# Row 0 of a fused attention and feed-forward kernel: the first half of the queries goes to the feed-forward layer ahead of the second half's masks, exponentials and last scores

## The chip, the core and the metric

The kernel runs on one core of a Trainium2 chip. The metric is the device time in microseconds (us) of one launch. The core has a matrix engine (TensorE, here PE), a vector engine (VectorE, DVE), a scalar engine (ScalarE, ACT), GpSimd (POOL) and SyncE (SP); the last two issue most of the DMA transfers here. Each engine takes its instructions in the order in which they were written, and waits on semaphores for the others.

## What is computed

The reference is attention with two kinds of masks, followed by a two-layer feed-forward network with a squared ReLU:

```python
B, H, S, D = 8, 8, 576, 64
scores = q @ k.transpose(0, 1, 3, 2) / sqrt(D)
rel = pos[:, None] - pos[None, :]
mask_plain = (rel >= 0) & (rel < 32)                       # heads 0 to 3
mask_dil = (rel >= 0) & (rel < 128) & (rel % 4 == 0)       # heads 4 to 7
attn = softmax(where(mask, scores, -1e9))
x = (attn @ v).transpose(0, 2, 1, 3).reshape(B * S, H * D) # 4608 tokens of 512
out = maximum(x @ w_in, 0) ** 2 @ w_out                    # 512 -> 2048 -> 512
```

## The kernel before

The attention works row by row of the batch (8 rows of 576 queries), the feed-forward part in chunks of 512 tokens. Nothing is scheduled by a planner: the order of the calls in the source is the order of the instructions on each engine. While one chunk goes through the feed-forward layers, the next row's attention is woven in between by `pump(n)`, which advances a generator of feed-forward work by n small steps. In the first layer two steps are one tile: four matmuls of 128x288 or 128x512 into one PSUM bank (line 291), a ReLU by ACT into `rt` (line 300), and a square by DVE into `g` (line 314 for row 0).

Row 0 has no chunk before it, so its attention stands alone, in the lines around 911 to 966. It is done in halves: the first 288 queries and the last 288. `mm1_first_gen` runs the first layer on row 0 in the same halves: eight tiles on the first half (tiles 0 to 7, which read columns 0 to 287 of `xr`), then eight on the second half, from tile 8 on, and so forth, 32 tiles in all.

The steps of row 0, with the lines that the profile names:

- Scores and exponentials: PE adds a bias that masks (`bias_of`, line 631, two matmuls of 128x288) to the scores (`s_sliding_one`, line 638, six matmuls), and `softmax` (line 619) has ACT write the exponential into one of eight units of `AT`. `s_first(hp, half)` does all three for two sliding heads and one half of the queries. Units 0 to 3 are the sliding heads, by pair of heads and half: (0,0), (0,1), (1,0), (1,1). Units 4 to 7 are the dilated heads; 4 and 6 are the first half, 5 and 7 the second. The exponentials of 5 and 7 are masked afterwards by two DVE products (line 940).
- Products with V: `av_dilated(0, t, a, ...)` (line 720, eight matmuls) gives half t of two dilated classes; `av_sliding(0, xs, m, ...)` (line 693, four matmuls for each m) gives blocks of 96 queries, m = 0 to 2 for the first half and 3 to 5 for the second. After each, DVE normalises from PSUM: a reciprocal (line 676) and a product (line 677) into `y` or `x`. V itself is cast by POOL (lines 218, 222, 235).
- Transposes: `x_dilated` (line 757) and `x_sliding` (line 742) turn a half of `y` and `x` by PE into PSUM, and ACT copies it into `xr` (lines 760 and 749, two copies each). The first layer's matmuls read `xr`: `x_sliding` is the last thing that a half needs.

PSUM is one tile of eight banks. `bank()` hands out banks 0 to 3 in turn (the first layer's tiles), `pair()` hands out pairs of banks in turn from the list `pairs`, for all of the attention. Row 0 uses all four pairs until the first layer begins; from there on the attention has only pairs 2 and 3 (banks 4 to 7):

```python
    pairs[:] = [2, 3]
    turns["pair"] = 0
    pending.append(mm1_first_gen())
    turns["bank"] = 2
```

A pair is written again only after whoever read its last content is done. The loads of `w_out` are issued by POOL (`load_w_out`, line 197), behind the casts and loads that POOL has before them; the two that the change's lines hold keep their place there.

## Time and profile before

| What | Value |
|---|---|
| Median of 3 runs | 299.29 us (298.81 to 299.5) |
| Profiled execution | 299.97 us, of which the span is 298.2 us |
| Granted PE clock, mean | 1.00 |
| Busy: PE, DVE, ACT, POOL | 96%, 68%, 59%, 33% |
| DMA | 45.59 MB, mean 153 GB/s |
| First tile of the first layer starts | 19.59 us |
| First layer runs without a gap | 22.96 to 36.68 us |

All times inside a profile count from the start of the span of one profiled execution; the launch takes about 1.8 us more than the span. In a line of the timeline the first number is the start, the second the time from the first start to the last end of the group; what stands in brackets is the idle time of the engine just before it, and what ended it. A line of the chain of waits gives the start, the duration, and the work or wait that held up the end. PE's matmuls are pipelined, so the rows of neighbouring matmuls overlap.

### The profile page before, as it was taken

To read this page: it belongs to the slowest core of one execution; us is meant where nothing else is said; L and a number is where in the kernel's file an instruction comes from. 1 tells how busy PE (TensorE), PEld (TensorE's weight loads), DVE (VectorE), ACT (ScalarE), POOL (GpSimd) and SP (SyncE) were. 2 spreads that over 40 slices of the span, in tenths; PEclk is the share of its full clock that TensorE was granted. 3 is DMA by queue.
4 is the path that set the end of the run, shared out by engine and by line. 5 is a ranking of instruction groups with operands and counts; after the bars stand their busy time and mean duration, and the time that the engine had idled before them with its cause. 6 is when DMAs were issued, how large, how long until landed. Compare 5 with 4: busy or idle time off the path is not lost.

```text
span 298.2 us, 7125 instructions
## 1 busy us (share of the span) xinstructions
PE 287.3 (96%) x2880; PEld 203.0 (68%) x2880; DVE 202.5 (68%) x371; ACT 176.4 (59%) x331; POOL 98.0 (33%) x154
## 2 busy tenths in 40 slices
PE   3999999999999999999999999999999999999995
PEld 2779854555555587646889987558755875785584
DVE  7786646778734898499588967896779624723652
ACT  1668854878538774857555648564766166425611
POOL 8492019406707245560655029209400000000000
PEclk9999999999999999999999999999999999999999
DMA  7999998799699878999999899979133230003013
GB/s 128 220 201 213 213 208 169 178 181 257 137 213 253 179 157 154 209 236 200 168 217 256 154 169 194 263 179 153 73 92 24 40 143 0 0 2 142 3 35 106
DMA packets 73969, 45.59 MB, mean 153 GB/s; under 512 B 56720, under 2 KB 67600, under 8 KB 73744
## 3 DMA queue, kind: packets, MB, share of 16 engines
q1 hardware_dynamic: 66544, 31.37, 48.0%
q0 software_dynamic: 7248, 13.63, 25.7%
q8 instruction: 22, 0.36, 0.5%
q10 hardware_dynamic: 144, 0.13, 0.1%
q14 instruction: 11, 0.09, 0.1%
HBM read 36.83 MB, written 16.52 MB: 179 GB/s over the span
## 4 chain that ended last, share of the span: by engine, by line
PE 81%; DMA 7%; DVE 4%; issue 2%; POOL 2%; SPq 1%; ACT 1%; POOLq 0%
PE PS L291 38%; PE PS L443 24%; PE PS L332 9%; DMA sv<-in_v_dram 5%; PE PS L720 3%; DMA ns<-in_k_dram 2%; PE PS L693 2%; PE PS L638 2%; PE PS L653 1%; POOL vp L218 1%; PE PS L742 1%; DVE AT L623 1%; POOL vp L222 1%; ACT AT L619 1%; SPq L168 1%
## 5 line engine op out<-in xcount | busy, mean ns | idle before, releaser
L291 PE MATMUL PS<-xr,wi 128*128 128x512 f16 (+3 forms) x704 | 133.5, 341 | 0.3 <-ACT xr L749 0.3
L300 ACT ACTIVATE rt<-PS 128x512 f16<-128x512 f32 (+2 forms) x160 | 88.5, 557 | 42.6 <-PE PS L291 39.7
L291 PEld LDWEIGHTS <-wi 128*128 128x128 f16 x704 | 75.8, 113 | 38.5 <-issue 0.4
L325 DVE TENSOR_TENSOR g<-rt 128x1024 f16<-128x1024 f16 (+1 forms) x64 | 46.1, 720 | 28.5 <-ACT rt L300 28.3
L619 ACT ACTIVATE AT<-PS 128x576 f16<-128x576 f32 x64 | 38.5, 652 | 14.8 <-PE PS L638 7.3
L443 PEld LDWEIGHTS <-S 128*128 128x128 f16 x448 | 42.8, 98 | 5.8 <-issue 0.3
L443 PE MATMUL PS<-T,S 128*128 128x256 f16 x336 | 39.5, 273 | 0.0
L443 PEld LDWEIGHTS <-g 128*128 128x128 f16 x336 | 32.2, 98 | 5.3 <-issue 0.2
L332 PE MATMUL PS<-wo,g 128*128 128x512 f16 x128 | 33.1, 379 | 0.0
L235 POOL CAST vd<-sd 128x512 f16<-128x512 f32 x32 | 23.9, 769 | 23.9 <-DMA sd<-in_v_dram 21.0
L443 PE MATMUL PS<-wo,g 128*128 128x256 f16 x224 | 26.4, 273 | 0.0
L218 POOL CAST vp<-sv 128x512 f16<-128x512 f32 x24 | 16.8, 700 | 24.2 <-DMA sv<-in_v_dram 20.0
L677 DVE TENSOR_TENSOR y<-PS,rcp 72x512 f16<-72x512 f32 (+1 forms) x32 | 22.0, 686 | 1.1
L623 DVE TENSOR_TENSOR AT<-AT,maskp 128x1152 f16<-128x1152 f16 x14 | 14.8, 1057 | 9.7 <-ACT AT L619 9.7
L623 DVE TENSOR_TENSOR AT<-AT,maskd 128x1152 f16<-128x1152 f16 x14 | 11.3, 810 | 14.1 <-ACT AT L619 14.0
L222 POOL CAST vp<-sv 32x512 f16<-32x512 f32 (+1 forms) x24 | 17.0, 708 | 1.5
L677 DVE TENSOR_TENSOR x<-PS,rcp 96x512 f16<-96x512 f32 (+1 forms) x25 | 16.6, 665 | 0.9
L720 PEld LDWEIGHTS <-AT 128*128 128x128 f16 x256 | 12.1, 100 | 7.1 <-DVE y L677 1.6
L332 PEld LDWEIGHTS <-g 128*128 128x128 f16 x128 | 10.3, 97 | 8.0
L429 DVE TENSOR_TENSOR S<-g,S 128x1024 f16<-128x1024 f16 x14 | 10.7, 804 | 7.4 <-PE PS L443 7.4
L676 DVE RECIPROCAL rcp<-PS 96x8 f32<-96x8 f32 (+3 forms) x57 | 11.2, 196 | 5.2 <-PE PS L720 2.9
L443 PE MATMUL PS<-T,g 128*128 128x256 f16 x112 | 14.2, 273 | 0.0
(94 smaller groups left out, 284.5 us busy)
## 6 DMA issues: line engine op xcount, KB each, us to landing
out_dram<-c SPq DMA_DIRECT2D x12, 512.0 KB
sv<-in_v_dram SPq DMA_DIRECT2D x48, 96.0 KB, 4.9
sd<-in_v_dram SPq DMA_DIRECT2D x16, 288.0 KB
dp<-o SPq DMA_DIRECT2D x12, 288.0 KB, 3.9
wo<-in_moe_w_out_dram POOLq DMA_DIRECT2D x4, 512.0 KB, 13.7
n<-in_k_dram POOLq DMA_DIRECT2D x6, 288.0 KB, 6.5
n<-in_q_dram POOLq DMA_DIRECT2D x6, 288.0 KB, 7.3
dd<-in_k_dram POOLq DMA_DIRECT2D x6, 288.0 KB, 8.0
```

Source lines behind the costliest of these rows:

```text
L218: nc.gpsimd.tensor_copy(vp[b % 2][:, m : m + 2, :, 0:D], sv[:, m : m + 2, :, :])
L222: nc.gpsimd.tensor_copy(vp[b % 2][0:PADP, m:m1, :, 0:D], sv[P - PADP : P, m - 1 : m1 - 1])
L235: nc.gpsimd.tensor_copy(o, by_class(sd[:, t]))
L291: nc.tensor.matmul(ph[:, o : o + b - a], w_in_of(dmk, ffc), xr[:, dmk, a:b], start=(dmk == 0 and o == 0), stop=(dmk == NDM - 1 and o + b - ...
L300: nc.scalar.activation(rt, ph[:, 0:w], ACTF.Relu)
L325: nc.vector.tensor_mul(g[:, f2 : f2 + 2, o:TOKC], rt[:, :, o:TOKC], rt[:, :, o:TOKC])
L332: nc.tensor.matmul(po, g[:, ffc, o + t * P : o + (t + 1) * P], w_out_of(ffc), start=(ffc == 0), stop=(ffc == NFF - 1),)
L443: nc.tensor.matmul(po[t], lhs(j)[:, t * P : (t + 1) * P], rhs(j), start=j == 0 and not on_top, stop=j == HF - 1, skip_group_check=on_top,)
L619: nc.scalar.activation(AT[:, u + i, 0:UW], ps[:, :, 0 : UW // 2], ACTF.Exp, scale=scale)
L623: nc.vector.tensor_mul(AT[:, u : u + n, 0:UW], AT[:, u : u + n, 0:UW], mask,)
L677: nc.vector.tensor_tensor(out=x, in0=pv[:, :, :, 0:D], in1=rcp[0:w, 0:i, 0:j].unsqueeze(3).to_broadcast([w, i, j, D]), op=ALU.mult,)
L720: nc.tensor.matmul(pav[:, e, h * (D + 2) : h * (D + 2) + D + 1], AT[:, 4 + 2 * a + t, off : off + P], vd[b % 2][:, t, 2 * a + e, h, 0 : D ...
```

## The change

The order of the calls for row 0 is changed; no step is added or taken away, and the number of instructions of every kind stays as it is. The scores (0,1) are still computed before the first layer begins, but behind the first half's products and dilated transposes, and their exponential behind the first half's copies. The masks of units 5 and 7 move behind the first half's normalisations. The products of the second half, and the scores (1,1), come after the point at which the attention has only the pairs 2 and 3, between tiles of the first layer. Fourteen steps of the first layer (seven tiles) are pumped ahead of `x_sliding(0, 1)`, where there were eight (four tiles).

```diff
-    for u in (5, 7):
-        nc.vector.tensor_mul(AT[:, u, 0:UW], AT[:, u, 0:UW], maskd[:, 1])
+
     xs, ys, zs = [], [], []
     av_dilated(0, 0, 0, ys)
     s_first(1, 0)
     av_dilated(0, 0, 1, ys)
-    s_first(0, 1)
     av_sliding(0, xs, 0, 1)
     av_sliding(0, xs, 2)
     x_dilated(0, 0, ys, True)
-    s_first(1, 1)
+    s02 = pair()
+    bias_of(s02, biasp)
+    s_sliding_one(0, 0, 1, s02, True)
     x_sliding(0, 0, xs, True)
-    av_dilated(0, 1, 0, zs)
-    av_dilated(0, 1, 1, zs)
-    av_sliding(0, xs, 3)
     load_w_out(0)
     load_w_out(1)
     pairs[:] = [2, 3]
     turns["pair"] = 0
+
+    softmax(1, [s02], None)
+    for u in (5, 7):
+        nc.vector.tensor_mul(AT[:, u, 0:UW], AT[:, u, 0:UW], maskd[:, 1])
     pending.append(mm1_first_gen())
     turns["bank"] = 2
     pump(4)
+    av_dilated(0, 1, 0, zs)
+    s_first(1, 1)
+    pump(2)
+    av_dilated(0, 1, 1, zs)
+    pump(2)
+    av_sliding(0, xs, 3)
     av_sliding(0, xs, 4, 5)
+    pump(4)
     x_dilated(0, 1, zs, True)
-    pump(4)
+    pump(2)
     x_sliding(0, 1, xs, True)
```

## The prediction

> **What bounds the kernel now.** I read the shares of busy time first, then the chain that ended last, then TensorE's (PE's) idle time in stretches of 5 us, and last the timeline from 13 to 25 us, where the change lies.

> ```profile
> PE 287.3 (96%) x2880; PEld 203.0 (68%) x2880; DVE 202.5 (68%) x371; ACT 176.4 (59%) x331; POOL 98.0 (33%) x154
> ...
> PE 81%; DMA 7%; DVE 4%; issue 2%; POOL 2%; SPq 1%; ACT 1%; POOLq 0%
> ```

> PE is the bound. The stretches say where it is not: from 25 us on it idles in five of them only (4.69, 4.56, 4.90, 4.48 and 4.63 busy of 5.00, so 0.31 + 0.44 + 0.10 + 0.52 + 0.37 = 1.74 us in 270). The work moved by the change is the same before and after, so the time can only change by PE's idle time before 25 us, and by what of that is given back later. The chain of waits shows the seam: from 22.96 us the first layer runs without a gap.

> ```profile
> 18.91 0.21 DVE rcp L676
> ...
> 19.99 0.03 DVE y L677
> ...
> 20.80 0.42 DVE x L677
> ...
> 21.80 0.70 DVE x L677
> 22.50 0.04 issue
> 22.55 0.41 PE PS L742 x6
> 22.96 13.72 PE PS L291 x112
> ```

> 112 matmuls in 13.72 us are 0.1225 us each, 0.49 us for a tile of four. Tile 8, the first that needs the second half of the queries, stands at 22.96 + 16 x 0.1225 = 24.92. The timeline (start, duration) has the rows that I move:

> ```profile
> 13.35 0.60 PE L720 MATMUL PS<-vd,AT 128*128 128x65 f16 x8 [0.26 <-POOL vd L235]
> ...
> 14.83 0.65 ACT L619 ACTIVATE AT<-PS 128x576 f16<-128x576 f32 x1 [1.06 <-PE PS L638]
> ...
> 15.69 0.60 POOL L222 CAST vp<-sv 32x512 f16<-32x512 f32 x1
> ...
> 18.46 0.67 PE L720 MATMUL PS<-vd,AT 128*128 128x65 f16 x16
> 18.85 0.70 ACT L749 COPY xr<-PS 128x288 f16<-128x288 f16 x2
> 19.59 1.14 PE L291 MATMUL PS<-xr,wi 128*128 128x288 f16 x8 [0.30 <-ACT xr L749]
> 19.76 0.19 DVE L676 RECIPROCAL rcp<-PS 72x8 f32<-72x8 f32 x1
> 19.99 0.69 DVE L677 TENSOR_TENSOR y<-PS,rcp 72x512 f16<-72x512 f32 x1
> 20.28 0.90 ACT L300 ACTIVATE rt<-PS 128x288 f16<-128x288 f32 x2 [0.74 <-PE PS L291]
> 21.14 0.51 DVE L314 TENSOR_TENSOR g<-rt 128x288 f16<-128x288 f16 x2
> ```

> A normalisation (reciprocal, then product) takes 0.92 us (19.76 to 20.68); a relu 0.45; a square 0.22 to the next instruction. A group of bias and scores holds PE for 0.96 us (13.76 to 14.72). The eight matmuls at 13.35 took 0.60 us, while sixteen of that form took 0.67 at 18.46: before about 18.3 us PE runs at half rate, though the granted clock reads 1.00.

> **The first half, up to the first tile.** PE's order becomes values, all first-half products and the dilated transposes, then scores (0,1), then the sliding transposes. The third product of `av_sliding(0, 1)` needs the exponential of the scores (1,0), which ends at 15.48; PE gets there at 15.26, since the scores that lay in between have gone: 0.25 idle. `av_sliding(2)` would start at 15.8 but needs POOL's cast of the shared rows (15.69 + 0.60 = 16.29): 0.45 idle. Then its 0.22, transposes 0.47, bias and scores 0.96: 18.0. The sliding transposes (0.43) are done at 18.6, ACT's two copies (0.70, the first after 0.40) run 18.65 to 19.35, and the first tile starts at 19.1 with its first matmul and goes on at 19.4. Before it was 19.59, so the head start is 0.2 to 0.5 us. Nothing fills PE from 18.4 on; before, 20 products did. The masks of units 5 and 7 (two of 0.6 us on DVE) move to 17.7 to 18.9, where DVE is free: nothing. The exponential (0,1) follows the copies on ACT, 19.3 to 19.9, ahead of the first relu, which is not ready earlier: nothing. POOL and SP get the same instructions in the same order; the two loads of w_out that stand in the moved lines are queued behind POOL's own casts as before: nothing.

> **The second half, between the tiles.** Before, its three first products had three pairs of PSUM banks (2, 3, 0). Now they come after `pairs[:] = [2, 3]` and go round two: first dilated product on pair 2, scores (1,1) on 3, second dilated on 2, `av_sliding(3)` on 3, `av_sliding(4, 5)` on 2, then the transposes on 3 and 2. Each waits until its pair is read out, PE takes its instructions in order, and the tiles behind it wait too. Step by step:

> - Tiles 0 and 1 run to 20.3, the first dilated product (0.25) to 20.5. In DVE's order both squares stand ahead of its normalisation. The second relu ends at about 20.9, the squares at 21.2, so the normalisation runs 21.2 to 22.1.
> - PE meanwhile does scores (1,1) (about 0.5 at full rate) and tile 2, to 21.55. The second dilated product needs pair 2: 22.1. **0.55 idle.**
> - Its own normalisation, behind the square of tile 2, ends at 23.5. PE does tile 3 and `av_sliding(3)`, to 23.0; `av_sliding(4, 5)` needs pair 2: 23.5. **0.5 idle.**
> - Tiles 4 and 5, dilated transposes, tile 6, sliding transposes and tile 7 run to 26.2. ACT has, from the relu of tile 5 (24.95) on: 0.4, copies 0.65, relu 0.4, copies 0.7. It is done at 27.0, the first of the last two copies at 26.7. Only tile 7 stands between the sliding transposes and tile 8, where it was four tiles before. **0.65 idle** until tile 8 is under way, at 26.9 in effect.

> So 26.9 against 24.92: 2.0 us later. Counted the other way: idle 0.25 + 0.45 + 0.85 + 0.55 + 0.5 + 0.65 = 3.25 against 0.95 before (0.45 ahead of the first tile, 0.2, 0.3), less 0.45 because scores (1,1) now run at full rate: 1.85. I take 2.0.

> **What carries to the end.** From 36.7 us on the row-1 loads are fixed by POOL's queue and only gain slack. The 1.74 us of later idle end on DVE or ACT, which hang on PE's own progress, so I carry all; if half of it waited for data of fixed arrival, 0.9 would be absorbed and 1.1 left. The profiled execution took 299.97 us (span 298.2 and 1.8 around it); the median of the runs is 299.29 (298.81 to 299.5). 299.97 + 2.0 = 301.97; against the median, 301.3, which I predict.

> **Rival 1, slower still: the full rate comes later.** The rate changed at about 18.3 us after 3 us in which nearly all PE time was full-height products and bias matmuls; it had not changed by 13 us, although PE was 4.56 of 5 us busy from 5 on, mostly with 64-row transposes. In the new order the stretch from 15.1 to 18.5 holds 0.7 us idle, 0.9 of transposes and one bias group instead of two. If that is too little, tiles 0 and 1 run at 0.245 us a matmul (+0.98), the group after them loses some 0.4, part of it eaten by the waits: 1.0 more, 302.3. [...] On these rows I give it a third.
> [...]

> **Rival 2, faster: the head start wins.** If the first two relus and squares were done before the first dilated product (20.5), its normalisation would end at 21.5, just when tile 2 does, and the 0.55 and 0.5 would fall away; with the copies earlier by as much, tile 8 stands at about 24.6, that is -0.3: 299.0. It decides at one point: does DVE start that reciprocal before 20.7? It needs the first tile at 18.6, and ACT's copies end later. 5 in 100.

> **Rival 3, no change.** The idle time is only moved: the later waits absorb, or PE runs some groups faster than I have them, 1.5 us in all: 299.8. Also here: that the first half is not ahead at all. It speaks against both that the three waits follow from the bank order alone. 5 in 100.

> **How the numbers follow.** The forecast of 301.3 has 0.55 (of it 0.1 with part absorbed, down to 300.4), rival 1 0.35 (302.3, up to 302.9 with the scatter of the runs and a window more), rivals 2 and 3 0.05 each. The range 300.2 to 302.9 leaves out about 0.15. 0.2% (0.6 us) is about what a measurement of this kernel can tell from no change. Faster 0.05, within it 0.05, slower 0.90.

> **What would show it.** The first L291 at 19.1 to 19.4; waits of PE for DVE's y on L720 and on L693, about 0.5 each; a wait of L291 for ACT's xr on tile 8; the unbroken run of L291 shrinks from 112 to about 96 and starts near 26.9; the first L332 comes at 38.5 instead of 36.5 and everything behind is later by as much. Rival 1 shows as eight L720 in 0.6 us after 20 us. I am wrong if the second dilated product follows within 0.1 us of tile 2, or if the shift at 38 us is gone by 60.

## The result and the profile after

The changed kernel takes 302.51 us (median of 6 runs, 301.12 to 303.73), against 299.0 us (298.46 to 299.5) for the kernel before on the same chip: a ratio of 1.0104, 95% interval 1.008 to 1.0128, or 3.1 us (the medians lie 3.5 us apart). Runs that took over 1.5% longer than the fastest of their kernel are left out of medians and ratios; there are two, both of f2 (305.50 and 306.35 us). The profiled execution took 303.6 us with a span of 301.8; it is the second longest of the six, so that its profile shows more of the loss (3.6 us) than the ratio does.

PE still carries the time (the profile's first part, and the chain that ended last):

```profile
PE 290.2 (96%) x2880; PEld 203.8 (68%) x2880; DVE 203.0 (67%) x371; ACT 176.1 (58%) x331; POOL 98.6 (33%) x154
...
PE 83%; DVE 8%; DMA 5%; issue 1%; ACT 1%; POOL 0%; DVEq 0%; ACTq 0%
```

The 2880 matmuls are the same as before, and PE is busy with them for 290.2 us instead of 287.3. So by the profile's count 2.9 of the 3.6 us are matmuls that took longer, and only 0.7 is time in which PE stood idle.

The chain of waits from 12 to 46 us (start, duration, what held up the end) shows where the time went:

```profile
11.52 7.62 DMA wi<-in_moe_w_in_dram
...
19.18 2.10 PE PS L291 x8
...
22.57 1.08 PE PS L291 x4
...
28.09 0.30 ACT xr L749
...
28.74 11.80 PE PS L291 x95
40.54 0.43 PE PS L332 x2
```

The unbroken run of the first layer had 112 matmuls from 22.96 on; now it has 95 from 28.74 on, and the second layer begins at 40.54 instead of 36.68. So 3.86 us are lost ahead of it, and 3.6 of them reach the end. The second thing to see is the price of a matmul. PE's rows of the timeline:

```profile
19.18 2.10 PE L291 MATMUL PS<-xr,wi 128*128 128x288 f16 x8 [1.03 <-DMA wi<-in_moe_w_in_dram]
21.09 0.64 PE L720 MATMUL PS<-vd,AT 128*128 128x65 f16 x8
...
22.50 1.15 PE L291 MATMUL PS<-xr,wi 128*128 128x288 f16 x4
23.44 0.64 PE L720 MATMUL PS<-vd,AT 128*128 128x65 f16 x8
...
25.59 1.14 PE L291 MATMUL PS<-xr,wi 128*128 128x288 f16 x8
```

At 19.18 eight matmuls take 2.10 us, where they took 1.14 before, and take it again at 25.59. PE ran at half rate until 25.0 us; in the profile of before it had changed to full rate at 18.2. Both times are read from the spacing of the matmuls, because the profile's granted clock reads 1.00 at either rate until its first fall.

### The profile page after: what moved, and what is told of

Its sections match the earlier page's. It is cut to its first block, busy times and chain, and to the rows that moved or that the text cites. A ratio compares the mean times of both kernels' runs of the same rounds, so it can differ in the third digit from the quotient of the medians.

```text
span 301.8 us, 7121 instructions
## 1 busy us (share of the span) xinstructions
PE 290.2 (96%) x2880; PEld 203.8 (68%) x2880; DVE 203.0 (67%) x371; ACT 176.1 (58%) x331; POOL 98.6 (33%) x154
## 4 chain that ended last, share of the span: by engine, by line
PE 83%; DVE 8%; DMA 5%; issue 1%; ACT 1%; POOL 0%; DVEq 0%; ACTq 0%
PE PS L291 39%; PE PS L443 25%; PE PS L332 10%; PE PS L720 3%; DMA wi<-in_moe_w_in_dram 3%; DMA ns<-in_k_dram 2%; PE PS L693 2%; PE PS L653 2%; DVE AT L623 2%; DVE S L429 1%; PE PS L638 1%; DVE g L325 1%; ACT AT L619 1%; PE PS L742 1%; PE PS L757 1%
## 5 line engine op out<-in xcount | busy, mean ns | idle before, releaser
L291 PE MATMUL PS<-xr,wi 128*128 128x512 f16 (+3 forms) x704 | 136.3, 344 | 1.2 <-DMA wi<-in_moe_w_in_dram 1.0
L300 ACT ACTIVATE rt<-PS 128x512 f16<-128x512 f32 (+2 forms) x160 | 88.5, 557 | 45.9 <-PE PS L291 43.4
L291 PEld LDWEIGHTS <-wi 128*128 128x128 f16 x704 | 75.8, 114 | 40.7 <-DMA wi<-in_moe_w_in_dram 1.2
L619 ACT ACTIVATE AT<-PS 128x576 f16<-128x576 f32 x64 | 38.5, 652 | 14.9 <-PE PS L638 7.6
L332 PE MATMUL PS<-wo,g 128*128 128x512 f16 x128 | 33.1, 379 | 0.0
L235 POOL CAST vd<-sd 128x512 f16<-128x512 f32 x32 | 23.4, 755 | 21.5 <-DMA sd<-in_v_dram 20.9
L218 POOL CAST vp<-sv 128x512 f16<-128x512 f32 x24 | 18.3, 762 | 23.8 <-DMA sv<-in_v_dram 22.7
L677 DVE TENSOR_TENSOR y<-PS,rcp 72x512 f16<-72x512 f32 (+1 forms) x32 | 22.0, 687 | 1.1
L623 DVE TENSOR_TENSOR AT<-AT,maskp 128x1152 f16<-128x1152 f16 x14 | 13.4, 960 | 9.2 <-ACT AT L619 9.1
L720 PEld LDWEIGHTS <-AT 128*128 128x128 f16 x256 | 12.8, 102 | 7.7 <-DVE y L677 1.8
L429 DVE TENSOR_TENSOR S<-g,S 128x1024 f16<-128x1024 f16 x14 | 12.7, 946 | 7.4 <-PE PS L443 7.4
L677 DVE TENSOR_TENSOR x<-PS,rcp 96x512 f16<-96x512 f32 (+1 forms) x25 | 16.6, 666 | 0.9
L222 POOL CAST vp<-sv 32x512 f16<-32x512 f32 (+1 forms) x24 | 16.0, 668 | 1.5
L314 DVE TENSOR_TENSOR g<-rt 128x288 f16<-128x288 f16 x32 | 9.8, 308 | 9.7 <-ACT rt L300 9.5
L332 PEld LDWEIGHTS <-g 128*128 128x128 f16 x128 | 10.3, 98 | 8.0
L720 PE MATMUL PS<-vd,AT 128*128 128x65 f16 x256 | 14.2, 200 | 0.8 <-DVE y L677 0.4
(94 smaller groups left out, 287.3 us busy)
```

Source lines behind the costliest of these rows:

```text
L218: nc.gpsimd.tensor_copy(vp[b % 2][:, m : m + 2, :, 0:D], sv[:, m : m + 2, :, :])
L222: nc.gpsimd.tensor_copy(vp[b % 2][0:PADP, m:m1, :, 0:D], sv[P - PADP : P, m - 1 : m1 - 1])
L235: nc.gpsimd.tensor_copy(o, by_class(sd[:, t]))
L291: nc.tensor.matmul(ph[:, o : o + b - a], w_in_of(dmk, ffc), xr[:, dmk, a:b], start=(dmk == 0 and o == 0), stop=(dmk == NDM - 1 and o + b - ...
L300: nc.scalar.activation(rt, ph[:, 0:w], ACTF.Relu)
L332: nc.tensor.matmul(po, g[:, ffc, o + t * P : o + (t + 1) * P], w_out_of(ffc), start=(ffc == 0), stop=(ffc == NFF - 1),)
```

## The experiments

They were made to part two causes: the waits of the new order, and the late full rate. Each is compared with the kernel before on the same chip.

**Dense matmuls at the start (e1, e2, e3, e4).** All four have these lines ahead of the first load; nobody reads the result:

```diff
+    hot = S2.rearrange("p j t -> p (j t)")[:, 0:TOKC]
+    nc.vector.memset(hot, 0.5)
+    for i in range(8):
+        nc.tensor.matmul(PS[:, 6 + i % 2, :], hot[:, 0:P], hot, start=True, stop=True)
```

e1 is the old order with them:

> The old order with eight dense matmuls of 128x512 on a constant added at the start, while PE waits for its first data; nobody reads their result. They are to bring PE to full rate before its own work begins. Theory (the loss of the new order has two parts, 2.0 us from waits of PE and the rest from the full rate coming at 25.2 instead of 18.5 us): full rate well before 18 us, the unbroken run of the first layer ends about 1.0 us earlier than at 36.7, time 298.0 (0.997 of before). Rival A (the rate plays no part, all of the loss is the order): 299.0, no change. If the full rate is lost again during the transposes from 6 to 13 us, this run can't tell.

299.7 us, ratio 1.0000 (0.9986 to 1.0015). Its profile has the full rate from 17.6 us on again, so it doesn't tell the theories apart. e2 is the new order with them:

> The new order with the same eight dense matmuls at the start. Theory: the rate is full throughout, what stays is the waits of PE: about 2.0 us behind the old order with the same matmuls, so 300.0 (1.003 of before), 2 to 2.5 us less than the new order without them (302.5). Rival A (order alone): 302 to 302.5. Rival B (the rate alone makes the loss, the waits are hidden): the same time as the old order with the matmuls, 298.0.

301.35 us, ratio 1.0081 (1.0047 to 1.0115), more than the 300.0 of the theory. The busy times by stretch of its profile (length, PE busy, then the other engines; granted clock third from the right) show what the eight matmuls do:

```profile
4.40:7.70 3.30, 1.66 (x27) 0.98 (x25) 3.10 (x13) 0.00 (x0) 3.09 (x7) 0.98 1.03 175
7.90:14.50 6.60, 6.32 (x144) 4.80 (x141) 4.68 (x14) 4.85 (x8) 3.08 (x7) 0.51 1.11 223
14.70:20.00 5.30, 3.41 (x51) 2.39 (x50) 3.20 (x9) 2.91 (x7) 5.13 (x9) 1.00 1.23 199
```

They bring the full rate for one stretch, from 4.1 us on by the spacing of the matmuls; then it is lost at 7.6 us, after a stretch in which PE was busy for half the time while it waited for its next data (0.98 us for a load, 0.66 for DVE), and comes back at 14.4. In this execution the rate was full before the first tile, and still the second layer began at 38.47, that is 1.8 us later than in the profile of before: the order has a cost of its own. e3 adds a third pair of banks for the second half; `bank()` takes its turns from the list `banks` there, and both lists go back to the old ones behind `x_sliding(0, 1)`:

```diff
-    pairs[:] = [2, 3]
+    pairs[:] = [2, 3, 0]
+    banks[:] = [2, 3]
     turns["pair"] = 0
     ...
-    turns["bank"] = 2
+    turns["bank"] = 0
```

> The new order with the eight dense matmuls, and three pairs of PSUM banks for the second half's attention (pairs 2, 3 and 0, while the first seven tiles of the first layer use banks 2 and 3 alone). Takes away what makes PE wait for a pair at the second dilated product and at av_sliding(4, 5). Theory: those two waits of about 0.5 us each fall away, the wait of tile 8 for ACT's copies stays; 0.9 us less than the new order with the matmuls and two pairs, 299.1. Rival (PE waits there for DVE or ACT in another way, and the pairs don't matter): within 0.2 us of it, 300.0.

301.89 us, ratio 1.0075 (1.0058 to 1.0093): by time not to be told from e2. The two waits for DVE's y are gone from its profile, but the full rate came at 20.6 us there and at 14.4 in e2's, so the comparison mixes both causes.

e4 takes the first half of the change alone (the moved lines are shown where they now stand, not where they were taken out):

```diff
     softmax(1, [s02], None)
     ...
+    av_dilated(0, 1, 0, zs)
+    s_first(1, 1)
+    av_dilated(0, 1, 1, zs)
     load_w_out(0)
     ...
     pump(4)
     av_sliding(0, xs, 3)
     av_sliding(0, xs, 4, 5)
     x_dilated(0, 1, zs, True)
     pump(4)
     x_sliding(0, 1, xs, True)
```

> The first half as in the new order, with the eight dense matmuls; the second half's two dilated products and the scores (1,1) go back ahead of the first layer's first tile, where all four pairs are free, and four tiles stand ahead of the sliding transposes as in the old order. One part of the change alone. Theory: the second half's products are off pair 2, but the first tile starts later by the products: 0.7 us less than the whole new order with the matmuls, 299.3, and still 1.3 us behind the old order with them. Rival (the deferral of the second half makes all of the loss): as fast as the old order with the matmuls, 298.0.

301.49 us, ratio 1.0062 (1.0039 to 1.0085), where the theory had 299.3; half rate until 22.4 us in its profile. Inconclusive for the same reason as e3; h3 repeats it without the matmuls.

**Dense matmuls all along the first 13 us (f1, f2, g3).** Sixteen of 128x256 at the start and four to six ahead of seven later groups of transposes, scores and products, in a bank that is written next:

```diff
+    def dense(i, n):
+        for j in range(n):
+            nc.tensor.matmul(PS[:, i + j % 2, 0:HT], hot[:, 0:P], hot, start=True, stop=True)
+    dense(6, 16)
     load_sliding_v(0, 0, 2)
     ...
     s01 = pair()
+    dense(2, 4)
     s_dilated_one(0, 0, 1, s01)
```

f1 is the old order:

> The old order with dense matmuls of 128x256 on a constant put between row 0's first steps, all ahead of 13.3 us: sixteen at the start, then 4 to 6 at a time ahead of the transposes, scores and first products; nobody reads their result. Eight at the start alone had raised PE to full rate for one stretch of 3.4 us and then lost it. These are to hold the rate. Theory: if the rate is full from 14 us on at the latest in every run, the end of the first layer's unbroken run comes at 35.7 instead of 36.6, time 298.3 to 298.6 and less scatter between the runs than the 2 us of before; what the added matmuls cost ahead of 13.3 us is the uncertain part (0 to 0.7). Rival (the rate is lost again between them): 0.5 to 3 us slower than before, half-rate rows after 13.3 us.

300.27 us, ratio 1.0033 (1.0009 to 1.0057), slower where the theory had it faster. The rate was full from 6.4 us on in its profile, but the first product with V came at 15.0 instead of 13.35, and the second layer began at 37.79 instead of 36.68. f2 is the new order:

> The new order behind the same dense matmuls as the old order with them. Theory: with the rate held in both, what is left is the order's own cost, PE's waits: 1.9 to 2.2 us behind the old order with the same matmuls (300.3 to 300.6 if that one takes 298.4), the waits of PE for DVE's y at the second dilated product and at av_sliding(4, 5) about 0.5 each, and tile 8 for ACT's copies; scatter below 1.5 us. Rival A (the rate made the whole loss): equal to the old order with the matmuls within 0.3. Rival B (the rate made nothing of it): 3.1 us behind it, as the new order is behind the old one without the matmuls.

303.39 us (300.94 to 305.31), ratio 1.0111 (1.0078 to 1.0144). It is 2.3 us behind f1 by the ratios and 3.1 by the medians, so rival A is out, and the times alone don't tell the theory from rival B; the scatter of 4.4 us is about three times the 1.5 that was expected. The stretches of its profile show that the rate was not held:

```profile
9.60:13.00 3.40, 3.40 (x86) 2.40 (x82) 2.19 (x5) 2.49 (x4) 1.55 (x4) 1.00 1.15 208
13.00:16.30 3.30, 3.19 (x76) 2.36 (x76) 1.52 (x3) 1.68 (x3) 3.19 (x6) 1.00 1.14 212
16.30:19.70 3.40, 1.74 (x33) 1.23 (x32) 2.09 (x7) 0.96 (x3) 3.34 (x7) 0.97 1.25 206
19.80:26.50 6.70, 6.15 (x47) 3.78 (x46) 2.96 (x10) 3.13 (x7) 2.77 (x5) 0.51 1.12 214
26.60:30.00 3.40, 3.03 (x42) 2.57 (x39) 2.60 (x9) 2.38 (x8) 0.54 (x1) 1.00 1.05 206
```

PE had the full rate, was busy for only 1.74 of 3.40 us in the stretch ahead of the first tile, and lost it for 6.8 us (from 19.5 to 26.3, so the stretches as cut here end 0.2 us late), although it was busy again in 6.15 of 6.70. The old order behind the same matmuls kept it in its profile. So in this execution the full rate was not only put off but taken away. The longest gap there, 1.1 us, stands ahead of a matmul for which the profile shows no releaser. g3 has the old order and fewer of them (31; the text on record says 33):

```diff
-    dense(6, 16)
+    dense(6, 14)
     ...
     s01 = pair()
-    dense(2, 4)
+    dense(2, 2)
```

> The old order with fewer dense matmuls ahead of 13.3 us (14 at the start, then 2 to 4 at a time, 33 in all instead of 48 of 128x256). The larger dose held the full rate from 6.6 us on, but put the first product with V at 15.0 instead of 13.35 us and gave 1.0033 of before. Theory: half the dose delays it by 0.5 or less; if the rate holds, the first layer's run ends at 36.0 and the time is 298.7 (0.997 of before). Rival (too thin to hold the rate): 299.5 to 301, half-rate rows between 8 and 18 us.

302.78 us, ratio 1.0107 (1.0088 to 1.0125): the smaller dose did not hold the rate, PE was at half rate up to 16.3 us and the first product came at 16.7. As a faster kernel it came to nothing.

**Dense matmuls where the new order lets PE wait (g1, g2).**

```diff
     av_sliding(0, xs, 0, 1)
+    dense(2, 2)
     av_sliding(0, xs, 2)
     ...
     x_sliding(0, 0, xs, True)
+    dense(2, 3)
```

> The new order with five dense matmuls of 128x256 put where PE waits in it: two ahead of av_sliding(2), which waits for POOL, and three between the first half's sliding transposes and the first tile, which waits for ACT. Nobody reads their result and no other instruction moves. Theory (the new order's thin stretch from 15 to 19 us keeps PE at half rate for one or two stretches of 3.4 us more): with the stretch filled the rate comes as in the old order, by 18 to 19 us, and the time falls from 302.5 to 301.3, the waits of about 2.0 us alone (1.006 to 1.007 of before). Rival A (the rate has other causes, dense work there changes nothing): 302.5 or slower by the 0.2 that the matmuls may delay the transposes. Rival B (the waits cost nothing): 299.5.

301.55 us (300.83 to 302.25), ratio 1.0069 (1.0047 to 1.0092), as the theory had it: with five matmuls that compute nothing the changed kernel comes out 1.0 us faster, by the medians (302.51 to 301.55) and by the ratios. The two were measured apart, each against before beside it, and the intervals just overlap (1.0080 to 1.0092). The full rate came at 17.6 us in its profile. Only the first two of the five stood ahead of that, from 15.91 on; the other three began at 18.14, when PE was waiting for the weights anyway. The chain of waits has the order's cost with the rate in time:

```profile
22.67 0.70 DVE y L677
...
23.41 0.43 PE PS L693 x8
...
26.18 0.30 ACT xr L749
...
26.83 11.80 PE PS L291 x95
38.63 0.43 PE PS L332 x2
```

The second layer begins at 38.63, that is 1.95 behind before's 36.68. PE's waits in that stretch (total, times, longest) are those of the working:

```profile
PE PS L291 <- DMA wi<-in_moe_w_in_dram: 0.5, 1, 0.5
PE PS L693 <- DVE y L677: 0.4, 1, 0.4
PE PS L720 <- DVE y L677: 0.3, 1, 0.3
PE PS L291 <- ACT xr L749: 0.2, 1, 0.2
```

They count from the modelled end of the last matmul. From start to start, as the working counts, more is lost:

```profile
20.95 0.68 PE L291 MATMUL PS<-xr,wi 128*128 128x288 f16 x4
21.96 0.43 PE L720 MATMUL PS<-vd,AT 128*128 128x65 f16 x8 [0.34 <-DVE y L677]
...
22.72 0.29 PE L693 MATMUL PS<-vp,AT 128*128 128x65 f16 x4
23.41 0.43 PE L693 MATMUL PS<-vp,AT 128*128 128x65 f16 x8 [0.40 <-DVE y L677]
```

The tile at 20.95 takes 0.49 us, so the second dilated product comes 0.5 us late. Four products take 0.13 us, so `av_sliding(4, 5)` comes 0.6 us late. Tile 8 comes in two steps, its first matmul at 26.52 and the rest from 26.83 on, together 0.5 us late.

g2 is g1 with the third pair of e3:

> The same with three pairs of banks for the second half's attention (2, 3 and 0, the first seven tiles on banks 2 and 3 alone). Theory: the waits for pair 2 at the second dilated product and at av_sliding(4, 5) go, about 0.9 us less than the new order with the five matmuls: 300.4; what stays of the order's cost is tile 8 behind ACT's copies and the idle time ahead of the first tile. Rival (the pairs don't matter, DVE's chain of normalisations sets the pace of the second half with two pairs or three): within 0.3 us of it, 301.2, and the sliding transposes wait for x instead.

300.92 us, ratio 1.0047 (1.0026 to 1.0067), 0.6 us less than g1; the intervals overlap. Both waits for y are gone from the profile, and one of 0.3 us is there for what DVE does next:

```profile
PE PS L742 <- DVE x L677: 0.3, 1, 0.3
```

From the first tile to the second layer it takes 18.93 us (19.59 to 38.52) against 19.52 in g1, which fits the difference of the medians. So the bank pairs are probably a part of the cost, of about 0.6 us, though the times don't prove it. Behind them DVE sets the pace: in g2's chain it works from 22.78 to 25.54 without a pause, squares and normalisations, until the transposes can go.

**Each half of the change alone (h2, h3).** h2 is the old order up to the scores (0,1), with masks and exponentials where they were, and the new order from the pairs on:

```diff
-    s_first(1, 1)
     x_sliding(0, 0, xs, True)
-    av_dilated(0, 1, 0, zs)
-    av_dilated(0, 1, 1, zs)
-    av_sliding(0, xs, 3)
     ...
     pump(4)
+    av_dilated(0, 1, 0, zs)
+    s_first(1, 1)
+    pump(2)
     ...
```

> One part of the change alone, with no matmuls added: masks, scores (0,1), their exponential and the whole first half stand as in the old order; the second half's products, the scores (1,1) and the transposes stand as in the new one, on pairs 2 and 3, between tiles. Theory (the order's 2.0 us come from the second half's waits for pair 2 and for ACT; the late rate comes from the new first half, thin between 15 and 19 us): 2.0 us over before and no more, 301.5, with scatter like before's 2 us, and the profile shows the full rate by 19 us. Rival A (the new first half costs part of the 2.0): 300.5. Rival B (the scores (1,1) taken out of the stretch are enough to delay the rate): 302.5, like the whole change.

302.71 us (301.98 to 303.04), ratio 1.0095 (1.0069 to 1.0121): rival B. This part alone costs what the whole change costs, the late rate included (22.6 us in its profile). Without the scores (1,1) and the twenty products that stood ahead of the first tile, PE waits in the chain for DVE's x until 18.2 (0.32 us) and for ACT until 19.6 (0.49 us), and the first eight matmuls run at half rate:

```profile
18.22 0.50 PE PS L742 x4
...
19.14 0.41 ACT xr L749
...
19.59 2.14 PE PS L291 x8
```

h3 is e4 without added matmuls:

> The other part alone, with no matmuls added: the first half as in the new order, then the second half's dilated products and the scores (1,1) ahead of the first tile on all four pairs, and four tiles ahead of the sliding transposes as in the old order. Theory: the waits for pair 2 are gone, 1.2 us are left (the exponential (1,1) now comes behind ACT's copies, so av_sliding(3) and what follows it come later); 300.7 where the rate comes as before, 301.8 where it comes one stretch later, which the thin first half makes likely in some runs. Rival (the first half ahead is a gain by itself): 299.0 or less.

301.36 us, ratio 1.0051 (1.0031 to 1.0071), between the two values expected. PE waits 1.0 us for DVE's x at the dilated transposes there, and its profile has half rate until 21.9.

**A better use of a tile (h1).** The old order with one tile more ahead of `x_sliding(0, 1)`:

```diff
     x_dilated(0, 1, zs, True)
-    pump(4)
+    pump(6)
     x_sliding(0, 1, xs, True)
```

> The old order with five tiles instead of four ahead of x_sliding(0, 1) (pump(6) for the last pump(4)). PE waits there 0.3 us for DVE's last x; one tile more (0.49 us) covers that, and three tiles are left between it and tile 8, 1.5 us against the 0.7 of ACT's copies. Theory (what a pumped tile is worth depends on the wait it covers, not on its number): the unbroken run ends 0.3 us earlier, 299.3 where before takes 299.6 (0.999), hardly to be told from no change. Rival (the fifth tile delays the transposes for nothing): 0.2 us slower.

299.39 us against 299.86, ratio 0.9980 (0.9961 to 1.0000). PE's wait for x ahead of L742 is gone from the chain, and the unbroken run starts at 23.30 with 108 matmuls left, which is worth 0.15 us there; the rest of the 0.5 is within what runs differ by. It is the only version that comes out below before, and just at the edge of being told from it.

## Why the prediction was right or wrong

**The direction: right. The mechanism: right where the rate is in time.** The prediction forecast 2.0 us slower by PE's own waits, 301.3; the time is 302.51, inside the range and 1.2 above the value. The forecast is borne out by g1: the order's cost is 1.95 us in the profile and 1.0069, or 2.1 us, by the runs. Tile 8 is under way at 26.83 where the working had 26.9. The changed kernel itself lands near rival 1's 302.3. That the number lies inside the range is owed to rival 1, for which the range had been widened.

**What was mis-sized: rival 1.** The late rate was put down as a rival with a chance of a third. The runs show it as the second term of the sum: the difference between the change and g1 is 1.0 us in the medians and 1.9 in the two profiles (40.54 against 38.63; the one is the second slowest of its six runs, the other the second fastest). The sign given for it is there: eight matmuls of line 720 take 0.64 us at 21.09 and at 23.44. Five of six runs of the change lie above 302. The price of 1.0 was right for the median. That 1.0 was worked out for half rate that ends behind tiles 0 and 1 and the group after them. h2's profile has it so (22.6 us), the change's has not: there it lasted to 25.0, though PE was busy for all of the 5.82 us from 19.18 on. The "window more" at the range's upper end is a term that no run shows by itself; what the runs showed in its place is a full rate that comes 6.8 us later than before (25.0 against 18.2 in the profiles) and a median of 302.51.

e2 shows when the rate changes: it rose at 4.1 us by the spacing of the matmuls, and the granted clock, worked out from its means by stretch, fell at 7.55 and rose at 14.38, so the changes lie 3.4 and 6.8 apart. The full rate that lasts comes at another time in each kernel's profile (14.4 us in e2, 17.6 in g1, 18.2 in before, 20.6 in e3, 25.0 in the change); that the scatter of the runs has its cause there is not shown. f2 lost the full rate at 19.5 after a stretch with PE busy for 1.74 of 3.40 us.

**The waits one by one.** With the rate in time (g1), the second dilated product comes 0.5 us late (forecast 0.55) `av_sliding(4, 5)` 0.6 (forecast 0.5), and tile 8 is under way 0.5 late (forecast 0.65). In the changed kernel's own profile the first of these isn't there: the second dilated product follows tile 2 at once (23.44, after a tile at 22.50 that takes 0.94 at half rate). The prediction had named that as a sign that it is wrong, and for this execution it is: PE came to pair 2 so late that DVE was done with it, at 22.9. There most of the lost time is slower matmuls (2.9 of 3.6 us), and the waits are shorter by what the half rate covers: the two causes don't simply add up.

Of the three waits that were given for the first half, the time ahead of the first tile is there (1.03 us for 0.85); the exponential held up the weights of a product by 0.24 us and PE by hardly 0.1. The cast by POOL ended 0.65 us earlier in the profiled execution and held up nothing. The first tile began at 19.18, as forecast, but for another reason, and that is luck: its weights landed then, 7.6 us after their issue, when ACT's first copy had been ready for 0.6 us. The head start was thus taken by a load that the working had as long done.

**The halves.** The working gave 1.55 of the 3.25 us of idle time to the first half. h2 keeps the old first half and loses as much as the whole, so the second half's move is enough for the loss. The new first half is not free for that: h3, which has it with the second half's dilated products and scores ahead of the first tile, is 0.5% slower than before (1.0051). The two parts don't add up, and on top of the second half's move the first half's costs nothing that these runs can tell.

**Carry and rivals.** Of 3.86 us 3.6 reach the end: 0.4 is absorbed between 48 and 60 us, where PE had waited 0.31 before, and 0.2 is added later. "I carry all" is thus near enough here, but it is no rule: against the same profile of before, g1 brings 1.2 of 1.95 us to the end, h2 3.0 of 3.72 and h3 2.3 of 2.33. Rivals 2 and 3 are out: the interval begins at 1.008.

## What to carry to other kernels

Work that fills an engine while it waits for another has a value that its own duration doesn't show: the second half's products and scores covered the first half's chain over DVE and ACT (without them PE waited 0.32 and 0.49 us there in h2), and taken out of it they waited themselves, on fewer banks (0.34 and 0.40 us for DVE's y in g1). Before moving steps between tiles, count the buffers that are left there, and how long each stays full. Where the rate of a matrix engine changes during a kernel, as it did here at 18.2 us before and at 25.0 after, a reordering that keeps the work the same can still change its price: the first eight matmuls of the first layer took 2.10 us instead of 1.14. Filling the gaps with matmuls that nobody reads helps to tell the two apart.
